# Projections of a second attention: fp16 pairs with power-of-two scales in place of fp32r pairs

## The chip, the cores and the metric

The kernel runs on one NeuronCore of a Trainium2 chip. The metric is the device time of one execution in microseconds. Five engines work side by side and meet at semaphores: TensorE (PE, matmuls, with its weight loads shown apart as PEld), VectorE (DVE), ScalarE (ACT), GpSimd (POOL) and SyncE (SP), whose queue issues most DMAs. Each engine runs its instructions in the order in which they were written.

## What is computed

Three layers follow each other; the change is in the second.

```python
# 1: attention, 2 batches, 8 heads, 768 x 64: a window of 128 keys and 4 sink keys
scores = np.where(is_sink | in_window, scale * q @ k.T, -1e9)
x = softmax(scores) @ v                      # as (2, 768, 512)
# 2: four attention experts of 64 columns, causal, two of them taken per row
logits = x @ w_gate                          # 512 x 4
topk = np.argpartition(-logits, 2, axis=-1)[..., :2]
for e in range(4):
    q, k, v = x @ wq[e], x @ wk[e], x @ wv[e]   # 512 x 64 each
    ye = softmax(causal(q @ k.T / 8)) @ v @ wo[e]
    out += weight(topk == e) * ye
# 3: eight feed-forward experts, one per row, chosen by argmax and a sticky local gate
out[b, s] = p[e] * (np.maximum(x[b, s] @ w1[e], 0) @ w2[e])
```

The order of the logits decides which expert a row takes, so the products must be close to fp32.

## The kernel before

A row tile has 128 rows: 6 tiles in each of the 2 batches. For each tile, layer 1 works head pair by head pair (`p1_unit`): scores on PE, mask and maximum on DVE (L687), exponential on ACT (L697), transposes of P on PE (L721), P split in a high half on ACT (L724) and a low half on DVE (L728), both fp16, and three products with the split V on PE (L736 to L738). From the third tile on, the sink keys get a product of their own, the sink product (L838), fed by small copies (L706). `p1_tail` normalises the tile to x (L859, DVE, out of PSUM), transposes it (L401) and splits it into `xT`, high half on ACT (L407), low half on DVE (L311).

Precision comes from pairs: each operand a is kept as a high half and a low half a - high, and `mm3` (L306 to L308) adds three products: high by high, high by low, low by high. In layer 1 the pairs of P and V are fp16, and V is first scaled by a power of two (`v_scale`, `pow2`). In the projections of layer 2 (`p2_v` for the values and the four gate logits, `p2_qk` for queries and keys) and in layer 3 the pairs are fp32r, which need no scale.

The weights of layer 2 come in three DMAs into two buffers of the ring `wst`, wv, wq, then wk, whose load waits until wv has been read. `weights` splits each: four high halves on ACT (L455), four low halves on POOL (L457, a plain subtraction). DVE takes one maximum, over wv (L448), which with V's bound gives the scale of the projected values (`across`, `pow2`, `p2_scale`).

The order of all instructions is made before anything runs. Each piece of work is a task with an engine, an estimated duration, the tasks it needs, the buffers it takes and a priority; `Order.run` always picks the task that can start earliest, and by priority among equals, and writes it out. Where PE would wait by that plan early in the program, it writes in fill matmuls of 512 columns (L387, `spin`). Layer 2 starts 3.75 tiles after layer 1, so up to then layer 1, the loads and the weights are all there is. POOL makes V's halves for most tiles (L636, L639, L645), DVE and ACT for a few (L625, L629).

The expert weights of layer 3 come through a ring of pairs `w`. Before, its first five buffers were the memory of the layer-2 weights and of `xT`, free once the last projection was through (`spent`); five more and the memory of `wo` came later.

Of the kernel before, what the change touches and what calls it, by code (L numbers as in the profile page):

```python
# [179 lines left out]
D_TR = 0.109  # L180
# [19 lines left out]
def fused_kernel(  # L200
# [48 lines left out]
    front = ExitStack()  # L249
    work = front.enter_context(tc.tile_pool(name="work", bufs=1))  # L250

    x2d = dram.tile([T * C, DM], F32, name="x2d")
    banks = [psum.tile([128, 512], F32, name=f"bank{i}") for i in range(8)]

    def ring(pool, n, name, *tiles):
# [106 lines left out]

    wqk_h = fw.tile([128, KD, 4, 128], FR)
    wqk_l = fw.tile([128, KD, 4, 128], FR)
    wvg_h = fw.tile([128, KD, E1 * D + E1], FR)
    wvg_l = fw.tile([128, KD, E1 * D + E1], FR)
    wo_h = fw.tile([128, 2, XC], FR)
# [62 lines left out]
    def weights(prio):  # L430

        wmax = small.tile([128, KD], F32, name="wmax", bufs=1)
        wgn = fw.tile([128, KD, E1], F32, name="wgn")
        K["wgn"] = add("DMA", 0.5, lambda: nc.sync.dma_start(wgn, w_gate1.rearrange("(p j) e -> p j e", j=KD)), prio=prio)
        g = add("ACT", 0.08, lambda: nc.scalar.activation(wvg_h[:, :, E1 * D:], wgn, AF.Copy), deps=[K["wgn"]], prio=prio)
        K["wg"] = add("POOL", 0.15, lambda: nc.gpsimd.tensor_sub(wvg_l[:, :, E1 * D:], wgn, f32(wvg_h[:, :, E1 * D:])),
                      deps=[g], prio=prio)
        mw = []
        for n, (name, w) in enumerate((("wv", wv), ("wq", wq), ("wk", wk))):
            load("wst", name, 512 * E1 * D * 4, lambda t, w=w: nc.sync.dma_start(  # L440
                t.rearrange("p (e j c) -> p e j c", e=E1, j=KD), w.rearrange("e (p j) c -> p e j c", j=KD)), prio + n)
            dst = [t[:, :, :E1 * D] for t in (wvg_h, wvg_l)] if n == 0 else \
                [t[:, :, 2 * (n - 1):2 * n, :].rearrange("p j m c -> p j (m c)") for t in (wqk_h, wqk_l)]

            def src(name, j):
                return R[name].rearrange("p (e j c) -> p j e c", e=E1, j=KD)[:, j]
            if n == 0:
                mw = [add("DVE", d_v(KD * E1 * D), lambda: nc.vector.tensor_reduce(  # L448
                    wmax[:, 0:1], R["wv"], axis=AX.X, op=OP.max, apply_absolute_value=True), deps=[K["wv"]], prio=prio)]
                K["gw"] = across("gw", lambda: wmax[:, 0:1], mw, prio)  # L450
# [8 lines left out]
            join(ls + (mw if n == 0 else []), [name], prio + n)  # L459
            K[name, "s"] = ls + ([K["wg"]] if n == 0 else [])  # L460
        wov = wo.rearrange("(t e) j c -> t (e j) c", t=2)
# [41 lines left out]

    def across(key, m, deps, prio):

        def a0():
            m1 = small.tile([128, 1], F32, name="amax1")
            nc.vector.reduce_max(m1, m(), axis=AX.X)
            R[key, "m1"] = m1

        def a1():
            nc.tensor.transpose(R[key, "p"][:, :128], R[key, "m1"].to_broadcast([128, 128]), ident)

        def a2():
            g = fw.tile([128, 1], F32, name="max_" + "".join(str(c) for c in key))
            nc.vector.reduce_max(g, R[key, "p"][:, :128], axis=AX.X)
            R[key] = g
        t0 = add("DVE", 0.08, a0, deps=deps, prio=prio)
        t1 = add("PE", D_TR, a1, deps=[t0], acq=[("B", (key, "p"))], prio=prio)
        return add("DVE", 0.2, a2, deps=[t1], rel=[(key, "p")], prio=prio)  # L520

    def pow2(key, m, deps, prio):
        def f():
            s = consts.tile([128, 1], F32, name="s_" + "".join(str(c) for c in key))
            si = consts.tile([128, 1], F32, name="si_" + "".join(str(c) for c in key))
            g = small.tile([128, 1], F32, name="amaxg")
            m(g)
# [5 lines left out]
            R[key] = (s, si)  # L533
        K[key] = add("DVE", 0.95, f, deps=deps, prio=prio)

# [275 lines left out]
    def p1_tail(b, i, prio):  # L811
# [64 lines left out]
    def p2_scale(b, prio):  # L876

        pow2(("sw", b), lambda g: nc.vector.tensor_scalar(g, R["gv", b], R["gw"], float(DM), op0=OP.mult, op1=OP.mult),
             [K["gv", b], K["gw"]], prio)

    def p2_v(b, i, prio):
# [10 lines left out]
        def g():  # L892
            p = R["v2p", b, i]
            nc.scalar.activation(v2[b][0][:, i, :], p[:, :E1 * D], AF.Copy, scale=R["sw", b][0])
            nc.scalar.activation(lg1[b][:, i, :], p[:, E1 * D:E1 * D + E1], AF.Copy)

        def h():
            nc.vector.scalar_tensor_tensor(v2[b][1][:, i, :], R["v2p", b, i][:, :E1 * D], R["sw", b][0], v2[b][0][:, i, :],
                                           op0=OP.mult, op1=OP.subtract)
        t = add("PE", 12 * d_mr(260) + 0.08, f, deps=[K["xT", b, i]] + K["wv", "s"], acq=[("B", ("v2p", b, i))],  # L900
                prio=prio)
        K["v2p", b, i] = t
        K["lg1", b, i] = u = add("ACT", 0.412, g, deps=[t, K["sw", b]], prio=prio)
        K["v2", b, i] = add("DVE", d_v(256) + 0.064, h, deps=[u], rel=[("v2p", b, i)], prio=prio)
# [28 lines left out]
    def p2_qk(b, m, c, prio):  # L933
# [10 lines left out]
        t = add("PE", 12 * d_mr(CH) + 0.07, f, deps=[K["xT", b, i] for i in range(2 * c, 2 * c + 2)] + K["wq" if m < 2 else "wk", "s"],  # L944
                acq=[("B", ("qkp", b, m, c))] + ([("q2", ("q2", b, c))] if m == 0 else []), prio=prio)
# [458 lines left out]
    def sp(u, c, hf, pr=None, ahead=False):  # L1404
# [126 lines left out]
    def unit_end(u):  # L1531
# [232 lines left out]
```

## Time and profile before

| what | value |
|---|---|
| median of 3 runs | 441.61 us (439.83 to 442.22) |
| the profiled execution | 440.41 us |
| its span, first to last instruction | 438.6 us |
| granted TensorE clock, mean | 0.995 |
| PE, DVE, ACT, POOL busy | 420.7, 352.2, 323.1, 129.9 us |
| chain that ended last, by engine | PE 56%, DVE 16%, issue 16%, ACT 6%, DMA 3% |

A busy share is an average over the whole span. Layer 1 starts alone, both attentions run together up to about 217 us, then come the last rows and the routing, and from about 265 us the expert layer. The rows in the section after the change are read stage by stage.

### The profile page before, as it was taken

The page shows a single profiled execution, that of the slowest core. Times are in us where ns is not written, and L with a number is a line of the kernel's source. Part 1 is how long each engine was busy: PE and PEld are TensorE (multiplying, and loading weights), DVE is VectorE, ACT ScalarE, POOL GpSimd, SP SyncE. Part 2 cuts the span into 40 slices and gives each one's busy share as a digit, 9 for nine tenths or more (in the row PEclk, how much of TensorE's full clock was granted, in tenths as well). Part 3 has the DMA queues.
Part 4 walks back from the last instruction along what each step waited for, and adds up shares of the span by engine and source line. Part 5 has one row for each costly group of instructions (what it writes and reads, how often), then busy time and mean ns, then how long its engine had stood idle before and what let it go on. Part 6 is the DMA issues. An engine that isn't in the chain of part 4 may idle for free.

```text
span 438.6 us, 10515 instructions
## 1 busy us (share of the span) xinstructions
PE 420.7 (96%) x3486; PEld 329.7 (75%) x3486; DVE 352.2 (80%) x1019; ACT 323.1 (74%) x759; POOL 129.9 (30%) x214
## 2 busy tenths in 40 slices
PE   8899999999999999999989999999999989999994
PEld 4679988769889779977966767655666767888883
DVE  3999696987889599868879887946779789998690
ACT  5799695975887598768556743936969789899780
POOL 8199921446002024110295104401102033100101
PEclk9999999999999999999999999999999999999999
DMA  8987251210210000100181025778565994100011
GB/s 173 174 189 195 53 118 49 49 50 1 75 50 1 25 2 2 49 1 27 55 315 41 26 73 172 259 240 266 193 212 188 340 390 143 49 26 24 2 50 53
DMA packets 58590, 48.28 MB, mean 110 GB/s; under 512 B 40863, under 2 KB 42399, under 8 KB 58528
## 3 DMA queue, kind: packets, MB, share of 16 engines
q1 hardware_dynamic: 56368, 40.72, 31.7%
q0 software_dynamic: 2160, 6.82, 4.6%
q8 instruction: 29, 0.48, 0.5%
q14 instruction: 33, 0.27, 0.2%
HBM read 86.58 MB, written 6.55 MB: 212 GB/s over the span
## 4 chain that ended last, share of the span: by engine, by line
PE 56%; DVE 16%; issue 16%; ACT 6%; DMA 3%; POOL 2%; SPq 1%; POOLq 0%; another core or an unknown queue 0%; ACTq 0%; DVEq 0%
PE bank L306 9%; PE bank L308 9%; PE bank L307 8%; PE bank L721 7%; PE bank L673 6%; DVE P L687 4%; PE bank L401 3%; DVE pT L728 3%; PE bank L1640 3%; DMA xg<-x2d,gix 2%; PE bank L738 2%; PE bank L736 2%; ACT P L697 2%; PE bank L1442 2%; PE bank L737 2%
## 5 line engine op out<-in xcount | busy, mean ns | idle before, releaser
L697 ACT ACTIVATE P<-P,nm 128x260 f32<-128x260 f32 (+4 forms) x160 | 84.0, 529 | 17.7 <-DVE nm L687 16.0
L728 DVE TENSOR_TENSOR pT<-bank,pT 128x512 f16<-128x512 f32 (+1 forms) x96 | 58.0, 627 | 13.6 <-ACT pT L724 13.1
L1421 DVE TENSOR_TENSOR w<-raw,w 128x1024 fp32r<-128x1024 f32 x44 | 52.9, 1220 | 12.7 <-ACT w L1413 12.4
L724 ACT ACTIVATE pT<-bank 128x512 f16<-128x512 f32 (+1 forms) x96 | 49.1, 550 | 6.8 <-PE bank L721 5.7
L1413 ACT ACTIVATE w<-raw 128x1024 fp32r<-128x1024 f32 x44 | 45.8, 1061 | 8.0 <-DMA raw<-in_moe_w_dram 6.8
L721 PE MATMUL bank<-ident,P 128*128 128x128 f32 x344 | 50.9, 280 | 0.7 <-ACT P L697 0.3
L687 DVE CUSTOM_DVE_ANT_0 P<-bank,mask 128x260 f32<-128x260 f32 (+1 forms) x96 | 36.4, 404 | 8.1 <-PE bank L673 8.0
L721 PEld LDWEIGHTS bank<-ident,P 128*128 128x128 f32 x344 | 38.5, 142 | 4.5 <-ACT P L697 2.4
L736 PEld LDWEIGHTS <-pT 128*128 128x128 f16 x344 | 31.0, 98 | 9.0 <-ACT pT L724 2.4
L1540 POOL DMA_INDIRECT out_dram<-yof,six x12 | 13.8, 1150 | 67.5 <-ACT yof L1537 66.3
L738 PEld LDWEIGHTS <-pT 128*128 128x128 f16 x344 | 30.7, 98 | 4.0 <-DVE pT L728 3.8
L673 PE MATMUL bank<-kT,qT 64*128 64x260 f32 (+1 forms) x192 | 31.2, 408 | 1.9 <-POOL kT L573 1.1
L737 PEld LDWEIGHTS <-pT 128*128 128x128 f16 x344 | 31.2, 99 | 1.1 <-issue 0.3
L697 ACT ACTIVATION_READ_ACCUMULATOR P<-P,nm 128x1 f32 x160 | 31.2, 195 | 0.0
L1462 POOL DMA_INDIRECT xgf<-x2d,gix x9 | 11.2, 1246 | 62.1 <-PE bank L1442 56.6
L306 PE MATMUL bank<-xT,wqk_h 128*128 128x256 f32 x96 | 28.8, 300 | 0.0
L401 PE MATMUL bank<-ident,raw 128*128 128x128 f32 x168 | 28.3, 289 | 0.2
L308 PE MATMUL bank<-xT,wqk_l 128*128 128x256 f32 x96 | 27.1, 282 | 0.0
L307 PE MATMUL bank<-xT,wqk_h 128*128 128x256 f32 x96 | 27.0, 281 | 0.0
L636 POOL TENSOR_SCALAR raw<-raw,s_sv 128x256 f32<-128x256 f32 x20 | 18.7, 946 | 27.1 <-DVE si_sv L532 17.7
L1421 DVE TENSOR_TENSOR xT<-raw,xT 128x1024 fp32r<-128x1024 f32 x17 | 20.6, 1216 | 6.9 <-ACT xT L1413 6.8
L401 PEld LDWEIGHTS bank<-ident,raw 128*128 128x128 f32 x168 | 20.4, 162 | 7.1 <-DVE nm L687 1.7
(444 smaller groups left out, 1319.9 us busy)
## 6 DMA issues: line engine op xcount, KB each, us to landing
raw<-in_moe_w_dram SPq DMA_DIRECT2D x104, 512.0 KB
qw<-in_moe_w_dram SPq DMA_DIRECT2D x64, 256.0 KB
raw<-in_v_dram SPq DMA_DIRECT2D x12, 256.0 KB
x2d<-x SPq DMA_DIRECT2D x12, 256.0 KB
raw<-in_q_dram SPq DMA_DIRECT2D x11, 256.0 KB
raw<-in_k_dram SPq DMA_DIRECT2D x11, 256.0 KB
raw<-in_moe_wv_dram SPq DMA_DIRECT2D x1, 512.0 KB
raw<-in_moe_wq_dram SPq DMA_DIRECT2D x1, 512.0 KB
```

The costliest lines, as they stand in the source:

```text
L306: nc.tensor.matmul(o, l[0], r[0], start=start, stop=False)
L307: nc.tensor.matmul(o, l[0], r[1], start=False, stop=False)
L308: nc.tensor.matmul(o, l[1], r[0], start=False, stop=stop)
L401: nc.tensor.transpose(p[:, j * 128:(j + 1) * 128], src(j), ident)
L673: nc.tensor.matmul(o, l, r, start=True, stop=True)
L687: nc.vector.tensor_tensor_reduce(p, s, sg["mask"], 0.0 if dead and st == 1 else -scale, gr["nm"] if si else 3.0e38, op0=OP.add, op1=OP.min ...
L697: nc.scalar.activation(p, p, AF.Exp, bias=gr["nm"], scale=-1.0, accum_out=sg["sum"]())
L721: nc.tensor.transpose(R[tk][:, j * 128:(j + 1) * 128], R[gr["P"]][:, c:c + 128], ident)
L724: nc.scalar.activation(R[sk_][0][:, :n * 128], R[tk][:, :n * 128], AF.Copy)
L728: nc.vector.tensor_sub(pl[:, :n * 128], R[tk][:, :n * 128], ph[:, :n * 128])
L1413: nc.scalar.activation(R["w", u, c, hf][0], R["raw", u, c, hf], AF.Copy)
L1421: eng.tensor_sub(wl[:, :, s_], R["raw", u, c, hf][:, :, s_], f32(wh)[:, :, s_])
```

## The change

The pairs of `xT` and of the weights wq, wk, wv and w_gate become fp16. That takes four things.

- **Scales.** Each weight gets a power of two from its own largest value (w_gate one of its own, beside wv's): a maximum over each weight on DVE, PE's transpose to bring it across the partitions (`across`, now straight from the column, for one or two columns), and a chain `pow2` each. The high halves on ACT take the scale as a factor; the low halves move from POOL to DVE as one fused operation, weight x scale - high.
- **x keeps V's scale.** The operation that normalises x no longer multiplies by V's inverse scale.
- **Undoing.** `p2_scale` makes small columns of products of the inverse scales, by batch (and, in the first batch, by V's two scales); the evictions of values, logits, queries and keys take them as a factor.
- **Memory.** `xT` and the layer-2 weights lie in a pool of their own, half as large, closed after the last projection (`turnover`). The ring `w` begins with two buffers of its own and gets three more at the turnover; the first conversions on POOL no longer wait for `spent`.

The number of matmuls and their shapes stay. The planner's estimates follow the new types (`d_mh` for `d_mr`, 0.55 for 0.95 for a `pow2`).

```diff
-        "xT": ring(fw, 2, "xT", ([128, KD, 2 * C], FR), ([128, KD, 2 * C], FR)),
+        "xT": ring(wx, 2, "xT", ([128, KD, 2 * C], F16), ([128, KD, 2 * C], F16)),
...
-    wqk_h = fw.tile([128, KD, 4, 128], FR)
+    wqk_h = wx.tile([128, KD, 4, 128], F16)
...
+            mw = add("DVE", d_v(KD * E1 * D), lambda name=name, n=n: nc.vector.tensor_reduce(
+                wmax[:, n + (n > 0):n + (n > 0) + 1], R[name], axis=AX.X, op=OP.max, apply_absolute_value=True), deps=[K[name]], prio=prio + n)
+            t = across(("g", name), lambda cols=cols: wmax[:, cols], [mw] + [mg] * (n == 0), prio + n, 2 if n == 0 else 1)
...
+            pow2(("s", name), lambda g, name=name: nc.vector.tensor_copy(g, R["g", name]), [t], prio + n, 2 if n == 0 else 1)
...
-                h = add("ACT", d_a(E1 * D), lambda name=name, j=j, h_=h_: nc.scalar.activation(h_, src(name, j), AF.Copy),
-                        deps=[K[name]], prio=prio + n)
-                ls.append(add("POOL", d_p(E1 * D), lambda name=name, j=j, h_=h_, l_=l_: nc.gpsimd.tensor_sub(
-                    l_, src(name, j), f32(h_)), deps=[h], prio=prio + n))
+                h = add("ACT", d_a(E1 * D), lambda name=name, j=j, h_=h_: nc.scalar.activation(
+                    h_, src(name, j), AF.Copy, scale=R["s", name][0][:, 0:1]), deps=[K["s", name]], prio=prio + n)
+                ls.append(add("DVE", d_v(E1 * D) + 0.064, lambda name=name, j=j, h_=h_, l_=l_: nc.vector.scalar_tensor_tensor(
+                    l_, src(name, j), R["s", name][0][:, 0:1], h_, op0=OP.mult, op1=OP.subtract), deps=[h], prio=prio + n))
...
-            nc.vector.scalar_tensor_tensor(x, R["O", 1, b, i].rearrange("p (h d) -> p h d", h=H),
-                                           R["se" if i < early(b) else "sv", b][1],
-                                           r[:, :, None].to_broadcast([128, H, D]), op0=OP.mult, op1=OP.mult)
+            nc.vector.tensor_tensor(x, R["O", 1, b, i].rearrange("p (h d) -> p h d", h=H),
+                                    r[:, :, None].to_broadcast([128, H, D]), op=OP.mult)
...
+            def f1(kind=kind, ud=ud):
+                nc.vector.tensor_scalar(ud[:, 0:2], R["s", "wv"][1], R[kind, b][1], None, op0=OP.mult)
+                nc.vector.tensor_mul(ud[:, 0:1], ud[:, 0:1], R["sw", b][0])
...
-        K["qk", b, m, c] = add("ACT", d_a(CH), lambda: nc.scalar.activation(dst(), R["qkp", b, m, c][:, :CH], AF.Copy),
-                               deps=[t] + ([K["qkp", b, 0, c]] if m == 1 else []), rel=[("qkp", b, m, c)], prio=prio)
+        K["qk", b, m, c] = add("ACT", d_a(CH), lambda: nc.scalar.activation(dst(), R["qkp", b, m, c][:, :CH], AF.Copy,
+                                                                            scale=undo(b, 2 * c, 2 + m // 2)),
...
-    bufs["w"] = [tuple(two(t, i) for t in wqk) for i in range(2)] + [(two(flat_(wvg_h)), two(flat_(wvg_l)))]
-    bufs["w"] += [tuple(two(flat_(t)) for t in p) for p in bufs["xT"]]
+    bufs["w"] = ring(fw, 2, "wa", ([128, 2, 512], FR), ([128, 2, 512], FR))
...
+    def turnover():
+        proj.close()
+        early_ = front.enter_context(tc.tile_pool(name="early", bufs=1, side="right", reuse_waits="tile"))
+        bufs["w"] += ring(early_, 3, "wb", ([128, 2, 512], FR), ([128, 2, 512], FR))
```

The planner's order moves with it. On DVE, before, from the end of the chain that makes the scale of the projected values (`s_sw`, `si_sw`) to the normalised x of the second tile (`raw_0_89`, L859) and on into the scores of the third:

```order
L531 TENSOR_SCALAR s_sw_725<-s_sw_725 128x1
L532 TENSOR_SCALAR si_sw_726<-amaxg 128x1
L859 SCALAR_TENSOR_TENSOR raw_0_89<-bank_82,si_se_459,r_0_1_231 128x512
L706 COPY skp_0_133<-P_0_104 128x3x8
L687 ISA P_0_101,nm<-bank_80,mask_172 128x260
```

The same place on DVE now, from the chain for wq's scale (`s_swq`) to the same x (`raw_0_92`, L871 in the new numbering); L460 are the low halves of the weights, L900 undo factors:

```order
L543 TENSOR_SCALAR s_swq<-s_swq 128x1
L544 TENSOR_SCALAR si_swq<-amaxg 128x1
L460 SCALAR_TENSOR_TENSOR wvg_l<-raw_0_86,s_swv,wvg_h 128x256
L900 TENSOR_TENSOR undo_se_233<-si_swq,si_se_469 128x1
L900 TENSOR_TENSOR undo_sv_234<-si_swq,si_sv_610 128x1
L460 SCALAR_TENSOR_TENSOR wvg_l<-raw_0_86,s_swv,wvg_h 128x256 x3
L465 SCALAR_TENSOR_TENSOR wvg_l<-wgn,s_swv,wvg_h 128x4x4
L460 SCALAR_TENSOR_TENSOR wqk_l<-raw_0_87,s_swq,wqk_h 128x256 x4
L871 TENSOR_TENSOR raw_0_92<-bank_85,r_0_1_236 128x512
```

Between the value scale's chain and the second tile's x stand now two more chains, a maximum over wq, the undo factors and nine low halves.

On POOL, before, from the low half of V's second tile (`v_1_98`, L645) on; L457 are the low halves of the weights:

```order
L645 TENSOR_TENSOR v_1_98<-raw_0_85,v_0_97 128x256 x2
L457 TENSOR_TENSOR wvg_l<-raw_0_83,wvg_h 128x256 x4
L457 TENSOR_TENSOR wqk_l<-raw_0_84,wqk_h 128x256 x4
L636 TENSOR_SCALAR raw_0_86<-raw_0_86,s_sv_598 128x256 x2
L639 CAST v_0_99<-raw_0_86 128x512
L645 TENSOR_TENSOR v_1_100<-raw_0_86,v_0_99 128x256 x2
L457 TENSOR_TENSOR wqk_l<-raw_0_83,wqk_h 128x256 x4
```

The same place on POOL now (L648, L651, L657 are L636, L639, L645 of before):

```order
L657 TENSOR_TENSOR v_1_101<-raw_0_88,v_0_100 128x256 x2
L648 TENSOR_SCALAR raw_0_89<-raw_0_89,s_sv_609 128x256 x2
L651 CAST v_0_102<-raw_0_89 128x512
L657 TENSOR_TENSOR v_1_103<-raw_0_89,v_0_102 128x256 x2
L648 TENSOR_SCALAR raw_0_89<-raw_0_89,s_sv_609 128x256 x2
L651 CAST v_0_96<-raw_0_89 128x512
```

The weights are gone from POOL, and V's tiles follow each other without a break.

## Rows read from the trace of the kernel before

**Rows 1.** The page: busy us, share of the span and instructions of each engine.

```profile
PE 420.7 (96%) x3486; PEld 329.7 (75%) x3486; DVE 352.2 (80%) x1019; ACT 323.1 (74%) x759; POOL 129.9 (30%) x214
```

**Rows 2.** Windows: stretch, length, busy us (instructions) by engine, granted clock, DMA share, GB/s.

```profile
core 0: us, PE busy (x) PEld busy (x) DVE busy (x) ACT busy (x) POOL busy (x), PEclk, DMA share, GB/s
20.00:40.00 20.00, 19.51 (x182) 15.88 (x181) 19.29 (x77) 19.26 (x64) 17.08 (x23) 1.00 0.86 200
40.00:60.00 20.00, 20.00 (x245) 18.60 (x245) 15.84 (x61) 15.82 (x51) 16.92 (x24) 1.00 0.36 86
160.00:180.00 20.00, 20.00 (x245) 17.08 (x243) 18.71 (x77) 17.95 (x63) 6.87 (x11) 1.00 0.04 15
31.00:46.00 15.00, 15.00 (x156) 14.40 (x155) 13.28 (x47) 13.74 (x47) 14.69 (x21) 1.00 0.59 148
```

**Rows 3.** PE in order of time: start, us, line, operands, shape, count.

```profile
26.84 1.03 PE L387 MATMUL bank<-v2h 128*128 128x512 f16 x4
29.16 0.81 PE L387 MATMUL bank<-v2h 128*128 128x512 f16 x3
31.53 1.04 PE L721 MATMUL bank<-ident,P 128*128 128x128 f32 x8
61.40 0.19 PE L736 MATMUL bank<-v,pT 128*128 128x64 f16 x1
61.43 0.19 PE L737 MATMUL bank<-v,pT 128*128 128x64 f16 x1
65.08 0.28 PE L306 MATMUL bank<-xT,wqk_h 128*128 128x256 f32 x1
66.03 0.28 PE L308 MATMUL bank<-xT,wqk_l 128*128 128x256 f32 x1
```

**Rows 4.** DVE in order of time, the operations that price the added ones.

```profile
13.96 0.68 DVE L585 TENSOR_REDUCE vmax<-raw 128x1 f32<-128x512 f32 x1
14.56 0.74 DVE L629 SCALAR_TENSOR_TENSOR v<-raw,s_se,v 128x512 f16<-128x512 f32 x1
20.56 0.29 DVE L516 TENSOR_REDUCE max_gv<-bank 128x1 f32<-128x128 f32 x1
21.36 0.14 DVE L595 COPY amaxg<-max_gv 128x1 f32<-128x1 f32 x1
22.25 0.68 DVE L311 TENSOR_TENSOR xT<-bank,xT 128x512 fp32r<-128x512 f32 x1
24.93 1.22 DVE L448 TENSOR_REDUCE wmax<-raw 128x1 f32<-128x1024 f32 x1
```

**Rows 5.** DVE beside POOL: order of time, and durations (ns, min/median/max) by line.

```profile
40.36 2.83 POOL L457 TENSOR_TENSOR wqk_l<-raw,wqk_h 128x256 fp32r<-128x256 f32 x4
41.14 0.72 DVE L923 TENSOR_TENSOR g_eq<-g_eq,tri 128x32 f32<-128x32 f32 x1
L923 DVE TENSOR_TENSOR g_eq<-g_eq,tri x6: 174/184/717, 41.1 to 212.4; 128x32 f32<-128x32 f32 x6
78.17 1.23 DVE L629 SCALAR_TENSOR_TENSOR v<-raw,s_sv,v 128x512 f16<-128x512 f32 x1
L636 POOL TENSOR_SCALAR raw<-raw,s_sv x20: 912/922/1357, 22.4 to 133.3; 128x256 f32<-128x256 f32 x20
```

**Rows 6.** DVE in order of time: waits of the first weights' stretch, idle before in brackets.

```profile
45.61 0.17 DVE L489 COPY wog<-bank 128x9 f32<-128x9 f32 x1 [0.73 <-PE bank L482]
46.50 0.17 DVE L489 COPY wog<-bank 128x9 f32<-128x9 f32 x1 [0.72 <-PE bank L482]
48.61 0.75 DVE L859 SCALAR_TENSOR_TENSOR raw<-bank,si_sv,r 128x512 f32<-128x512 f32 x1 [1.94 <-PE bank L838]
```

**Rows 7.** ACT groups: busy us, mean ns, idle before; with a scale and without.

```profile
L894 ACT ACTIVATE v2h<-bank,s_sw 128x256 f16<-128x256 f32 x12 | 5.5, 462 | 0.0
L947 ACT ACTIVATE k<-bank 128x256 f32<-128x256 f32 x12 | 4.6, 384 | 14.2 <-PE bank L308 14.2
```

**Rows 8.** Windows of PE alone around a wait for a gather: busy us (instructions), granted clock.

```profile
225.00:229.00 4.00, 2.26 (x20) 0.99 0.81 278
229.00:232.50 3.50, 3.50 (x25) 0.52 0.47 178
```

More of the change, by code (lines that the diff above doesn't have):

```diff
@@ L250, in fused_kernel @@
     work = front.enter_context(tc.tile_pool(name="work", bufs=1))
+    proj = ExitStack()
+    wx = proj.enter_context(tc.tile_pool(name="wx", bufs=1, side="right"))
     x2d = dram.tile([T * C, DM], F32, name="x2d")
@@ L430, in weights @@
     def weights(prio):
-        wmax = small.tile([128, KD], F32, name="wmax", bufs=1)
+        wmax = small.tile([128, 4], F32, name="wmax", bufs=1)
         wgn = fw.tile([128, KD, E1], F32, name="wgn")
         K["wgn"] = add("DMA", 0.5, lambda: nc.sync.dma_start(wgn, w_gate1.rearrange("(p j) e -> p j e", j=KD)), prio=prio)
[L435 to L438, printed above, removed]
+        mg = add("DVE", 0.09, lambda: nc.vector.tensor_reduce(
+            wmax[:, 1:2], wgn.rearrange("p j e -> p (j e)"), axis=AX.X, op=OP.max, apply_absolute_value=True), deps=[K["wgn"]], prio=prio)
         for n, (name, w) in enumerate((("wv", wv), ("wq", wq), ("wk", wk))):
@@ L501, in weights, with across @@
         join([K["wos", t] for t in range(2)] + [a], ["wo"], prio + 2)
-    def across(key, m, deps, prio):
+    def across(key, m, deps, prio, n=0):
         def a0():
@@ L511, in a1, with pow2 @@
         def a1():
-            nc.tensor.transpose(R[key, "p"][:, :128], R[key, "m1"].to_broadcast([128, 128]), ident)
+            for j in range(max(n, 1)):
+                col = m()[:, j:j + 1] if n else R[key, "m1"]
+                nc.tensor.transpose(R[key, "p"][:, j * 128:(j + 1) * 128], col.to_broadcast([128, 128]), ident)
         def a2():
-            g = fw.tile([128, 1], F32, name="max_" + "".join(str(c) for c in key))
-            nc.vector.reduce_max(g, R[key, "p"][:, :128], axis=AX.X)
+            w = max(n, 1)
+            g = fw.tile([128, w], F32, name="max_" + "".join(str(c) for c in key))
+            nc.vector.reduce_max(g, R[key, "p"][:, :128 * w].rearrange("p (n c) -> p n c", n=w), axis=AX.X)
             R[key] = g
[L518 to L522, printed above, removed]
+        t0 = deps if n else [add("DVE", 0.08, a0, deps=deps, prio=prio)]
+        t1 = add("PE", D_TR * max(n, 1), a1, deps=t0, acq=[("B", (key, "p"))], prio=prio)
+        return add("DVE", 0.2 * max(n, 1), a2, deps=[t1], rel=[(key, "p")], prio=prio)
+    def pow2(key, m, deps, prio, n=1):
         def f():
-            s = consts.tile([128, 1], F32, name="s_" + "".join(str(c) for c in key))
-            si = consts.tile([128, 1], F32, name="si_" + "".join(str(c) for c in key))
-            g = small.tile([128, 1], F32, name="amaxg")
+            s = consts.tile([128, n], F32, name="s_" + "".join(str(c) for c in key))
+            si = consts.tile([128, n], F32, name="si_" + "".join(str(c) for c in key))
+            g = small.tile([128, 2], F32, name="amaxg")[:, :n]
             m(g)
@@ L533, in f @@
             R[key] = (s, si)
-        K[key] = add("DVE", 0.95, f, deps=deps, prio=prio)
+        K[key] = add("DVE", 0.55, f, deps=deps, prio=prio)
     def halves(b, i):
@@ L876, in p2_scale, with f2, undo, undone @@
     def p2_scale(b, prio):
-        pow2(("sw", b), lambda g: nc.vector.tensor_scalar(g, R["gv", b], R["gw"], float(DM), op0=OP.mult, op1=OP.mult),
+        pow2(("sw", b), lambda g: nc.vector.tensor_scalar(g, R["gv", b], R["g", "wv"][:, 0:1], float(DM), op0=OP.mult, op1=OP.mult),
              [K["gv", b], K["gw"]], prio)
+        for kind in (["se"] if early(b) else []) + ["sv"]:
+            ud = small.tile([128, 4], F32, name=f"undo_{kind}{b}", bufs=1)
+            R["undo", b, kind] = ud
+            def f1(kind=kind, ud=ud):
+                nc.vector.tensor_scalar(ud[:, 0:2], R["s", "wv"][1], R[kind, b][1], None, op0=OP.mult)
+                nc.vector.tensor_mul(ud[:, 0:1], ud[:, 0:1], R["sw", b][0])
+            def f2(m, kind=kind, ud=ud):
+                nc.vector.tensor_mul(ud[:, 2 + m:3 + m], R["s", "wk" if m else "wq"][1], R[kind, b][1])
+            K["undo", b, kind, 0] = add("DVE", 0.14, f1, deps=[K["sw", b], K[kind, b], K["s", "wv"]], prio=prio)
+            for m in range(2):
+                K["undo", b, kind, 1 + m] = add("DVE", 0.07, lambda m=m, f2=f2: f2(m), deps=[K[kind, b], K["s", "wk" if m else "wq"]], prio=prio + 1)
+    def undo(b, i, n):
+        kind = "se" if i < early(b) else "sv"
+        return R["undo", b, kind][:, n:n + 1]
+    def undone(b, i, n):
+        return K["undo", b, "se" if i < early(b) else "sv", n]
     def p2_v(b, i, prio):
@@ L1422, in sp @@
         after = [K["ga", 1]] if u == 0 and (c, hf) == (3, 1) else []
-        h = K["wh", u, c, hf] = add("POOL" if ahead else "ACT", 1.06 if ahead else d_a(1024) + 0.055, hi, deps=[K["ld", u, c, hf]] + (spent + [K["routed", JE]] * c if ahead else [K.get(("wh", 0, 1, 1))] * (u == 0 and c == 2)),
+        h = K["wh", u, c, hf] = add("POOL" if ahead else "ACT", 1.06 if ahead else d_a(1024) + 0.055, hi, deps=[K["ld", u, c, hf]] + ([K["routed", JE]] * c if ahead else [K.get(("wh", 0, 1, 1))] * (u == 0 and c == 2)),
                                     acq=[("w", ("w", u, c, hf))], prio=pr)
```

38 lines of the change are left out of this document (23 added, 15 removed).

## The prediction

> **What bounds the kernel now.** I read the page's busy shares first, then the table of windows, then VectorE (DVE) and TensorE (PE) in order of time around 10 to 50 us. On the page PE is busy 96% of the span [rows 1], but that says nothing on the stage that the change touches. The windows split it [rows 2]. From 40 to 60 and from 160 to 180 us PE is busy all 20.00 us, DVE 15.84 and 18.71: there PE is the bound, and a matmul that gets shorter is worth its whole saving. From 20 to 40 us DVE has 19.29 and ScalarE (ACT) 19.26 of 20 us: there whatever is added to them pushes the rest. The change takes PE time out of the first kind of stretch and puts DVE work into the second, so the two are priced apart.
>
> **What it takes from PE.** The projections are 12 value products and 24 query and key products of 12 matmuls each, 432 in all. From 65.08 to 66.03 us nine fp32r matmuls in a row start 0.12 us apart [rows 3]. No fp16 matmul of 256 columns is in the trace. The nearest are the fill matmuls of 512 columns (three take 0.81 us, four 1.03: 0.22 each) and the 64-column products of the attention, 0.03 us apart, each with a weight load of its own, so the load of 128 columns doesn't hold them [rows 3]. A line through both, 0.03 + 192 x 0.00042, gives 0.11 for 256 columns. So 0.01 is saved on each, 4.3 us in all. The bounds are 0, if something else than the type sets the 0.12, and 0.013 each, if an fp16 matmul goes by its columns alone (half of 0.22 less the rounding). I take 0.01, and of the 432 only those that run where PE is the bound: 72 (two value and four query and key products) lie in the stretch that DVE will hold up, the other 360 save 3.6 us.
>
> The rows give 0.22 per fp16 matmul of 512 columns. The Trainium skill (TensorE: Matmul & The Clock Gate, Back-to-back issue gap) gives 81 ns at 128 columns and 131 ns at 512 as the sustained spacing with a weight load each; an estimate between these two figures is 98 ns at 256, by which 360 matmuls would save 7.9 us and the sum below would be +0.9. At 512 columns the row is far above 131 ns, so the row decides.
>
> **What it adds to DVE.** Before, GpSimd (POOL) made the low halves of the weights; now DVE does, and takes the maxima and makes the scales. Counted from the order, priced by the durations of DVE in order of time [rows 4] (each operation starts about 0.08 us before the one ahead of it ends, 13.96 + 0.68 against 14.56):
> - two more maxima over a 1024-wide weight tile, 1.22 us each: 2.4
> - three more power-of-two chains of six one-column operations, 0.89 us from 21.36 to 22.25: 2.7
> - maxima over three more transposed columns, 0.29 less the overlap: 0.6
> - eight small operations for the undo factors, 0.07 to 0.19 each as in the chain: 0.9
> - twelve low halves of 256 columns. The 512-column form (L629 at 14.56) takes 0.74 less 0.08; 512 columns more cost a maximum 0.54 (1.22 against 0.68), so 256 fewer save 0.27: 0.39 each, 4.7.
>
> That is 11.3 us, and it all stands ahead of the attention output of the third tile (L859, at 48.61 us before [rows 6]). The DVE pieces in the section on the change show it: from the scale chain to the output of the second tile there was nothing, now there are two more chains, nine low halves and more. PE gets 14 more fill matmuls there (39 against 25 up to the first sink product): the useful work waits for DVE.
>
> What takes it up: DVE stood idle three times there until PE was through, 0.73 + 0.72 + 1.94 = 3.4 us [rows 6]; that goes first. And PE works ahead: up to the first sink product it has now done 12 transposes more, 0.11 each (eight take 1.04 [rows 3]), 1.3 us. 11.3 - 3.4 - 1.3 = 6.6.
>
> **The shared port.** DVE beside POOL in order of time shows POOL in DVE's way [rows 5]. From 40.36 to 43.19 POOL runs four weight subtractions end to end. DVE's small two-input operation of the gate at 41.14 takes 0.72 us and ends as the second of them ends; the same line has a median of 184 ns over the program and a maximum of 717. The change works both ways here. It removes the 12 subtractions. Some 16 such short operations (sink copies, gate) stand in the stretch, held by up to 0.53 each; half of that is 4 us that could come back. But POOL's preparation of V moves up into the gap (POOL has 14.69 of 15 us from 31 to 46 us [rows 2]), and the order puts four tiles of it there back to back, so I count 1.0. Against it, the twelve new DVE operations and the gate's all read two SBUF tiles. The one row of that form beside POOL work is L629 at 78.17: 1.23 us, 0.49 more than 0.74, while POOL's next operation is held in turn (at most 1357 ns, median 922). The bounds for thirteen are 0 and a whole POOL operation of 0.75 each, 9.8; the row would give 6.4. I take half of it, 3.2: the key weights' four come late, perhaps after POOL's work, and no row shows several in succession.
>
> That row has a hold of 0.49. The Trainium skill (SBUF — State Buffer, Who interferes with whom) says that a DVE instruction with two SBUF inputs contends with a GpSimd one that reads SBUF, and that the second to issue is blocked until the first is through. Strictly taken it would be the upper bound, 9.8 in place of 3.2; that is the fourth case below.
>
> **Smaller edits.** A scale from a tensor makes ACT's evictions longer: 462 ns with it, 384 without [rows 7]. 24 query and key evictions, 12 of the logits and 13 weight pieces make 49 x 0.08 = 3.9 us of ACT. From 40 us on ACT is busy 79 to 90% [rows 2] and this lies beside PE's work; the weights' 1.0 us lies beside DVE's longer stretch. Cost 0, up to 1. The x output loses one factor but still reads PSUM at a pass an element: 0. On SP's queue the loads of wk and wo now wait for DVE's last read of wv and wq, with a key tile and V tiles behind them; the maximum over wk stands on DVE behind the second split of x, long after its load: 0. The expert stage has as many weight buffers as before, split in another way, two of them free earlier; its loads are not moved: 0, by 1 us either way.
>
> **Sum.** 6.6 - 1.0 + 3.2 - 3.6 = +5.2 us. The profiled execution took 440.41 us for a span of 438.6, so 445.6 for one like it; the median of the runs shown is 441.61, 1.2 above it, which gives 446.8.
>
> **The rivals**, all on that median. A measurement of this kernel tells about 0.5%, 2.2 us, from no change.
> - *A, the forecast (0.45):* DVE is late in the first 50 us, with some holds at the port: 442.5 to 450.5, middle 446.8.
> - *B, they cancel (0.22):* the new operations are not held and 4 us come back: 6.6 - 4.0 - 3.6 = -1.0, 440.6. For it: POOL must let DVE in between two of its operations; against it: L629's row.
> - *C, faster (0.17):* its place is DVE from 25 to 48 us, its mechanism that POOL's subtractions were what made DVE slow there. If two thirds of the possible holds go, 5.5 us, no new ones come and a matmul saves 0.013: 6.6 - 5.5 - 4.7 = -3.6, 438.0. It decides once DVE reaches the third tile's output less than 4.9 us (3.6 + 1.3) later than before. Against it: V's preparation reads SBUF as the subtractions did, and stands in their place.
> - *D, far slower (0.11):* every new operation waits out one of POOL's, 9.8, and PE, starved meanwhile, loses its clock: from 225 to 229 us PE was busy 2.26 of 4 us, and from 229 to 232.5 the granted clock is 0.52 [rows 8], near the lower of its two levels, 1.2 of 2.4 GHz; half of 3.5 us is 1.7. 6.6 - 1.0 + 9.8 + 1.7 - 3.6 = +13.5, 455.1.
> - *E, the matmuls don't get shorter (0.05):* 0.12 stays, as for fp32r: 6.6 - 1.0 + 3.2 = +8.8, 450.4.
>
> **How the numbers follow.** A, D and E are slower by over 0.5%: 0.61. B is within: 0.22. C is faster: 0.17. The time is A's, 446.8. The range leaves out the lower part of C and most of D: 439.5 to 452.5. The slower cases alone would have 442.5 to 455.
>
> **What would show it.** The output of the third tile comes at 55 to 61 us in place of 48.61. The new low halves take 0.47 us where POOL is idle and up to 1.2 beside it. Projection matmuls start 0.11 apart. PE is full again right after, the first gather for the experts comes about 5 us later than before, and the stage behind it is as it was. I am wrong if PE stays full from 31 to 46 us (15.00 of 15.00 before [rows 2]), or if the spacing is under 0.10.

## The result, and the profile after

The changed kernel takes 445.31 us (median of 6 runs, 444.78 to 447.92), the kernel before 441.61 beside it: ratio 1.010, 95% interval 1.006 to 1.014. It is slower by about 4.5 us, inside the forecast. The profiled execution has a span of 446.1 us (before 438.6); it is the longest of its runs, so a second trace of the same kernel, 443.2 us long and the shortest of its ten, is read beside it.

The page and the windows of the first trace, against [rows 1, 2]:

```profile
PE 423.1 (95%) x3503; PEld 322.7 (72%) x3503; DVE 363.6 (81%) x1066; ACT 327.3 (73%) x759; POOL 122.7 (27%) x201
```

```profile
20.00:40.00 20.00, 16.93 (x142) 11.28 (x140) 19.38 (x71) 13.36 (x36) 16.07 (x19) 0.93 0.67 151
40.00:60.00 20.00, 19.11 (x216) 16.54 (x215) 18.39 (x73) 16.59 (x48) 9.44 (x14) 0.98 0.56 116
31.00:46.00 15.00, 11.59 (x74) 7.80 (x73) 14.55 (x48) 9.44 (x27) 14.54 (x19) 0.89 0.71 171
160.00:180.00 20.00, 19.96 (x260) 15.72 (x260) 19.32 (x66) 18.09 (x58) 5.64 (x9) 1.00 0.04 15
36.00:42.00 6.00, 3.93 (x21) 2.58 (x21) 6.00 (x16) 3.16 (x10) 5.85 (x7) 0.72 0.35 102
246.00:250.00 4.00, 4.00 (x29) 3.23 (x27) 3.86 (x13) 3.79 (x12) 0.00 (x0) 0.63 0.01 4
```

From 31 to 46 us PE is busy 11.59 us instead of 15.00, ACT 9.44 instead of 13.74, and DVE goes up to 14.55: DVE is the bound there, and the others wait for it. At 160 us PE is as full as before. Two stretches at a lower granted clock, 0.72 and 0.63, stand out. These are means over a stretch: from 38 to 40 us the clock is 0.50, the lower of its two levels (1.2 of 2.4 GHz). The second trace has the same idle time and neither stretch:

```profile
31.00:46.00 15.00, 11.13 (x85) 7.51 (x82) 14.59 (x49) 10.17 (x28) 14.08 (x17) 1.00 0.79 174
36.00:42.00 6.00, 4.22 (x30) 2.99 (x30) 6.00 (x18) 3.15 (x9) 5.78 (x7) 1.00 0.59 142
246.00:250.00 4.00, 3.96 (x55) 3.10 (x54) 3.80 (x11) 4.00 (x13) 0.00 (x0) 1.00 0.02 4
```

DVE in order of time in the first trace, the new work (before: [rows 4, 6]):

```profile
31.25 0.47 DVE L453 COPY amaxg<-max_gwv 128x2 f32<-128x2 f32 x1
31.75 0.41 DVE L540 TENSOR_SCALAR amaxg<-amaxg 128x2 f32<-128x2 f32 x1
34.51 0.15 DVE L540 TENSOR_SCALAR amaxg<-amaxg 128x1 f32<-128x1 f32 x1
36.13 1.26 DVE L460 SCALAR_TENSOR_TENSOR wvg_l<-raw,s_swv,wvg_h 128x256 f16<-128x256 f32 x3
37.60 2.42 DVE L460 SCALAR_TENSOR_TENSOR wqk_l<-raw,s_swq,wqk_h 128x256 f16<-128x256 f32 x4
39.95 0.68 DVE L871 TENSOR_TENSOR raw<-bank,r 128x512 f32<-128x512 f32 x1
47.89 1.68 DVE L460 SCALAR_TENSOR_TENSOR wqk_l<-raw,s_swk,wqk_h 128x256 f16<-128x256 f32 x4
59.58 0.69 DVE L871 TENSOR_TENSOR raw<-bank,r 128x512 f32<-128x512 f32 x1
```

The second tile's x comes at 39.95 instead of 29.37 us, the third's at 59.58 instead of 48.61 [rows 6]. The second tile's before:

```profile
29.37 0.75 DVE L859 SCALAR_TENSOR_TENSOR raw<-bank,si_se,r 128x512 f32<-128x512 f32 x1
```

The chain for wv's two scales (from 31.25) takes 1.80 us; the chains for wq and wk, 0.89 and 0.88. What PE and ACT do meanwhile, in order of time:

```profile
31.69 2.54 PE L389 MATMUL bank<-v2h 128*128 128x512 f16 x11
34.06 0.60 PE L403 MATMUL bank<-ident,raw 128*128 128x128 f32 x4
37.51 0.37 PE L308 MATMUL bank<-wvg_h,xT 128*128 128x260 f16 x1 [2.84 <-ACT qT L409]
```

```profile
33.10 1.71 ACT L458 ACTIVATE wvg_h<-raw,s_swv 128x256 f16<-128x256 f32 x4 [2.50 <-DVE s_swv L543]
35.27 1.70 ACT L458 ACTIVATE wqk_h<-raw,s_swq 128x256 f16<-128x256 f32 x4 [0.26 <-DVE s_swq L543]
36.88 0.57 ACT L409 ACTIVATE qT<-bank 128x512 f32<-128x512 f32 x1
```

PE runs 11 fills in a row, four transposes, and is idle for 2.84 us. ACT is idle for 2.50 us until the scale of wv is there, and the query's eviction (L409) stands in its queue behind the high halves of wv and wq.

The span splits at the first gather for the experts. On POOL before, in the first trace after and in the second:

```profile
218.15 1.21 POOL L1462 DMA_INDIRECT xg<-x2d,gix  x1 [1.40 <-DVE no L1268]
```

```profile
223.45 1.21 POOL L1492 DMA_INDIRECT xg<-x2d,gix  x1 [2.09 <-DVE no L1300]
```

```profile
222.63 1.21 POOL L1492 DMA_INDIRECT xg<-x2d,gix  x1 [2.09 <-DVE no L1300]
```

The gather is 5.3 and 4.5 us late. Behind it, up to the end of the span, lie 220.4 us before, 222.7 in the first trace after and 220.5 in the second. So the loss is in the front. The 2.2 us behind it in the first trace are not in the second, so the change alone doesn't bring them.

### The profile page after: what moved, and what is told of

Same layout as the page of the kernel before. It is cut to its first block, busy times and chain, and to the rows that moved or that the text cites. A ratio compares the mean times of both kernels' runs of the same rounds, so it can differ in the third digit from the quotient of the medians.

```text
span 446.1 us, 10614 instructions
## 1 busy us (share of the span) xinstructions
PE 423.1 (95%) x3503; PEld 322.7 (72%) x3503; DVE 363.6 (81%) x1066; ACT 327.3 (73%) x759; POOL 122.7 (27%) x201
## 4 chain that ended last, share of the span: by engine, by line
PE 51%; DVE 17%; issue 16%; DMA 6%; ACT 5%; SPq 2%; POOL 2%; POOLq 0%; another core or an unknown queue 0%; ACTq 0%; DVEq 0%
PE bank L308 8%; PE bank L310 8%; PE bank L309 7%; PE bank L685 7%; PE bank L733 6%; DVE pT L740 4%; DMA raw<-in_moe_w_dram 4%; DVE P L699 3%; PE bank L403 3%; PE bank L1677 2%; PE bank L750 2%; PE bank L748 2%; PE bank L749 2%; DMA qw<-in_moe_w_dram 1%; SPq L1667 1%
## 5 line engine op out<-in xcount | busy, mean ns | idle before, releaser
L1451 DVE TENSOR_TENSOR wb<-raw,wb 128x1024 fp32r<-128x1024 f32 x25 | 30.3, 1219 | 8.6 <-ACT wb L1443 8.5
L685 PE MATMUL bank<-kT,qT 64*128 64x260 f32 (+1 forms) x192 | 30.2, 409 | 1.2 <-issue 1.1
L1443 ACT ACTIVATE wb<-raw 128x1024 fp32r<-128x1024 f32 x25 | 26.4, 1062 | 2.6 <-DMA raw<-in_moe_w_dram 1.3
L648 POOL TENSOR_SCALAR raw<-raw,s_sv 128x256 f32<-128x256 f32 x20 | 19.0, 960 | 33.1 <-DVE si_sv L544 22.8
L699 DVE CUSTOM_DVE_ANT_0 P<-bank,cmask 128x384 f32<-128x384 f32 (+3 forms) x48 | 24.3, 527 | 4.4 <-PE bank L685 4.3
L308 PE MATMUL bank<-xT,wqk_h 128*128 128x256 f16 x96 | 26.2, 273 | 0.3 <-DVE wog L497 0.3
```

The costliest lines, as they stand in the source:

```text
L308: nc.tensor.matmul(o, l[0], r[0], start=start, stop=False)
L685: nc.tensor.matmul(o, l, r, start=True, stop=True)
L699: nc.vector.tensor_tensor_reduce(p, s, sg["mask"], 0.0 if dead and st == 1 else -scale, gr["nm"] if si else 3.0e38, op0=OP.add, op1=OP.min ...
L1443: nc.scalar.activation(R["w", u, c, hf][0], R["raw", u, c, hf], AF.Copy)
L1451: eng.tensor_sub(wl[:, :, s_], R["raw", u, c, hf][:, :, s_], f32(wh)[:, :, s_])
```

## Experiments

The prediction's theory: DVE's added work, less what is taken up, costs more than the shorter matmuls give. The rivals: the loss is somewhere else (expert buffers, the planner's order, ACT's wait), the matmuls give nothing, POOL's subtractions had slowed DVE. A time difference below is a ratio times 441.6.

### All of the new work, fp32r operands

```diff
-    wqk_h = wx.tile([128, KD, 4, 128], F16)
+    wqk_h = fw.tile([128, KD, 4, 128], FR)
...
-    bufs["w"] = ring(fw, 2, "wa", ([128, 2, 512], FR), ([128, 2, 512], FR))
+    bufs["w"] = [tuple(two(t, i) for t in wqk) for i in range(2)] + [(two(flat_(wvg_h)), two(flat_(wvg_l)))]
```

> The changed kernel with its projection operands back in fp32r and the expert buffers of before, and all of the new work on the weights (maxima, scales, DVE low halves) kept. If the shorter matmuls are what the change gains, the projections start 0.12 us apart again and the time is that of the changed kernel plus about 4.3 us: 445.3 + 4.3 = 449.6, ratio to before about 1.018. If the type gains nothing on the path (rival E), it stays at 445. If the new expert buffers cost the 2 us that the stage behind the first gather has become longer in the profile after, it would be 447.5 and that stage as short as before.

Measured: 454.99 us, ratio 1.032 (1.028 to 1.036): +14.1. So the fp16 operands, with the buffers and the order that go with them, are worth some 10 us beside this work, over twice what was expected. Up to the first gather it is 8.0 (230.62 against 222.63). The other 3.6 lie behind the gather, where there are no projections: this trace is the longest of its four and has a granted clock of 0.79 from 246 to 254 us, so part of them is this execution's, and the rest may be the buffers' or the order's. PE in order of time, here and in the second trace after, shows what the type changes:

```profile
73.34 0.37 PE L306 MATMUL bank<-wvg_h,xT 128*128 128x260 f32 x1
73.55 0.28 PE L307 MATMUL bank<-wvg_l,xT 128*128 128x260 f32 x1
73.67 0.28 PE L308 MATMUL bank<-wvg_h,xT 128*128 128x260 f32 x1
```

```profile
71.31 0.27 PE L308 MATMUL bank<-wvg_h,xT 128*128 128x260 f16 x1
71.42 0.27 PE L309 MATMUL bank<-wvg_l,xT 128*128 128x260 f16 x1
71.53 0.27 PE L310 MATMUL bank<-wvg_h,xT 128*128 128x260 f16 x1
```

Within a group the starts are 0.12 and 0.11 apart. But the first interval of an fp32r group is 0.21, of an fp16 group 0.11.

### fp16 operands without the new work

The weights are not scaled here: POOL subtracts as before the change, and one maximum is left.

```diff
...
-                    h_, src(name, j), AF.Copy, scale=R["s", name][0][:, 0:1]), deps=[K["s", name]], prio=prio + n)
-                ls.append(add("DVE", d_v(E1 * D) + 0.064, lambda name=name, j=j, h_=h_, l_=l_: nc.vector.scalar_tensor_tensor(
-                    l_, src(name, j), R["s", name][0][:, 0:1], h_, op0=OP.mult, op1=OP.subtract), deps=[h], prio=prio + n))
...
+                    h_, src(name, j), AF.Copy, scale=1.0), deps=[K[name]], prio=prio + n)
+                ls.append(add("POOL", d_p(E1 * D), lambda name=name, j=j, h_=h_, l_=l_: nc.gpsimd.tensor_sub(
+                    l_, src(name, j), h_), deps=[h], prio=prio + n))
```

> The changed kernel's fp16 projections and nothing of its work on the weights: unscaled fp16 high halves on ACT, all twelve low halves on GpSimd as before the change, one maximum, no scales of the weights. Against the version with fp32r operands and all of that work (455.0) the fp16 operands were worth 9.7 us. If that gain doesn't depend on the work beside it: 441.4 - 9.7 = 431.7, and at least 434 by what the matmuls' starts alone give (7.2 us to the first gather). If the planner's new order or the moved buffers are what costs, and not DVE's work: 438 to 442, near the version with the fixed scale and GpSimd's low halves (441.7).

Measured: 437.35 us, ratio 0.991 (0.987 to 0.9945): -4.1, faster than both kernels, but short of the 431.7 expected. Its first gather:

```profile
214.97 1.21 POOL L1481 DMA_INDIRECT xg<-x2d,gix  x1 [1.72 <-DVE no L1289]
```

That is 3.2 us ahead of before. The intervals from one projection start to the next sum to 55.1 us before and 48.0 here. The short intervals ahead of the groups grow from 1.2 to 2.0 in all, so PE saves 6.3. Half of it arrives at the gather. (This trace is the shortest of its ten; 2.0 us of its lead lie behind the gather.) So what the type gives depends on what stands beside it: 4.1 us alone, about 10 beside the new work. The new work costs 8.3 us on fp16 operands (from -4.1 to +4.2, the mean of the two measurements of the change) and 14.1 on fp32r.

### A fixed scale, and POOL's subtractions back

A constant 2^10 instead of the maxima over wq, wk and w_gate and the three chains; the weights' own scale is left out:

```diff
-            pow2(("s", name), lambda g, name=name: nc.vector.tensor_copy(g, R["g", name]), [t], prio + n, 2 if n == 0 else 1)
...
-                    l_, src(name, j), R["s", name][0][:, 0:1], h_, op0=OP.mult, op1=OP.subtract), deps=[h], prio=prio + n))
+                    l_, src(name, j), WS, h_, op0=OP.mult, op1=OP.subtract), deps=[h], prio=prio + n))
```

> The changed kernel without the choice of the weights' scales: a fixed 2^10 stands in place of three maxima (2 x 1.21 and 0.17 us), their 0.42 + 0.28 + 0.27 us over the transposed columns, the three power-of-two chains (1.80 + 0.89 + 0.89) and about 1 us of undo operations; the twelve low halves stay on DVE. If DVE's work ahead of the second and third tile is the cause, about 7.5 us of it goes, ACT no longer waits 2.5 us for the first scale, the first projection starts at or before 35 us, PE has no idle stretch of 2.8 us and no half clock there: 438.5, between 437 and 441. If the low halves and their holds at the port are the larger part, 443 to 445. If the loss lies behind the first gather, 443.

Measured: 442.69 us, ratio 1.0007 (0.997 to 1.005): +0.3, some 4 us less than the changed kernel for about 7.5 us less of DVE work, of which wk's 2.2 stand where it had idle time and wv's low halves now meet POOL. Then wq's and wk's low halves back on POOL, unscaled:

```diff
+                if n:
+                    ls.append(add("POOL", d_p(E1 * D), lambda name=name, j=j, h_=h_, l_=l_: nc.gpsimd.tensor_sub(
+                        l_, src(name, j), h_), deps=[h], prio=prio + n))
+                    continue
```

> As the one with the fixed scale, and the eight low halves of wq and wk go back to GpSimd (subtractions of unscaled weights, as before the change); the value weights' stay on DVE. If DVE's time is all that counts, 8 x 0.45 = 3.6 us of DVE go, 1 to 2 of them on the path: 437. If GpSimd's subtractions were what slowed DVE (rival C), it is slower than the fixed scale alone by 1 to 4 us: 440 to 443.

Measured: 441.72 us, ratio 1.002 (0.999 to 1.005), not to be told from the fixed scale alone. Eight low halves less on DVE and eight subtractions more on POOL cancel within the noise, and this run doesn't part the two. But the version above has all its subtractions on POOL and is the fastest of all: they don't have to go for the kernel to get faster (rival C). What they cost is not shown. What is left on DVE is wv's low halves and the gate's, and they now fall beside POOL's sink values. DVE, and POOL, in order of time:

```profile
24.89 1.08 DVE L467 SCALAR_TENSOR_TENSOR wvg_l<-wgn,wvg_h 128x16 f16<-128x16 f32 x1
27.72 2.12 DVE L462 SCALAR_TENSOR_TENSOR wvg_l<-raw,wvg_h 128x256 f16<-128x256 f32 x2
```

```profile
24.90 1.03 POOL L623 TENSOR_TENSOR vbd<-vk,bdm 96x512 f32<-96x512 f32 x1
28.35 1.21 POOL L626 TENSOR_TENSOR vbd<-vbd,vbd 32x512 f16<-32x512 f32 x1
```

A 16-column operation takes 1.08 us, as long as the POOL operation beside it; the next two low halves take 0.83 and 1.37 us, where one takes 0.41 at its shortest. These five, with the four undo operations, occupy about 4.7 us; the version without scales, above, has all of them but two undo operations off DVE and is 5.0 us faster (from +0.9 to -4.1). By this pair, each microsecond of DVE at this place is about one of the whole.

### The planner's estimate

```diff
-        K[key] = add("DVE", 0.55, f, deps=deps, prio=prio)
+        K[key] = add("DVE", 0.95, f, deps=deps, prio=prio)
```

> The changed kernel with the planner's estimate for a power-of-two chain at 0.95 us as before the change, not 0.55 (the trace has 0.89 to 1.80). The work is the same and only the order moves. If the planner's too short estimate is what lets ACT wait 2.5 us for the scale and hold the query's evictions behind it, the stretch from 31 to 46 us gets fuller and the time falls by 1 to 3 us: 442.5 to 444.5. If the work itself is the cause, it stays within 1 us: 444.5 to 446.

Measured: 447.62 us, ratio 1.0145 (1.010 to 1.019). It doesn't get faster; the first gather is at 223.89, 0.4 and 1.3 us later than in the two traces of the changed kernel. The too short estimate is not the cause. It also shows what an order alone can do to this kernel: up to some 2 us. Every version here has an order of its own, so a difference of that size between two of them is no measure of the work.

### DVE's time by itself, at two places, and ACT's wait

Six maxima over weight tiles that nobody reads, in the kernel before: three each behind wv and wq; the same with ACT's high halves planned behind them; and all six behind wk.

```diff
+            dm = []
+            for i in range(3 if n < 2 else 0):
+                dm.append(add("DVE", d_v(KD * E1 * D), lambda name=name, c=3 * n + i: nc.vector.tensor_reduce(
+                    dmx[:, c:c + 1], R[name], axis=AX.X, op=OP.max, apply_absolute_value=True), deps=[K[name]], prio=prio + n))
```

> The kernel before with six more maxima over 1024-wide weight tiles on DVE, three behind the load of wv and three behind that of wq, 1.13 us each, 6.8 in all, that nothing waits for but the release of the two tiles. By the prediction's term, DVE's idle time (3.4) and PE's working ahead (1.3) take up 4.7 us: +2.1, 443.5. If nothing is taken up: +6.8, 448.2. The version with all of the change's work and no fp16 was 13.6 us slower for 13.9 us of DVE, which speaks for the second.

Measured: 447.42 us, ratio 1.016 (1.006 to 1.026): +7.0 for 6.8 us of DVE, with bounds of +2.6 and +11.3. The prediction's +2.1 lies below them: most of the work is not taken up. The first gather is at 223.83, 5.7 us late, and DVE shows the place:

```profile
27.91 3.46 DVE L454 TENSOR_REDUCE dmx<-raw 128x1 f32<-128x1024 f32 x3
33.55 1.21 DVE L454 TENSOR_REDUCE dmx<-raw 128x1 f32<-128x1024 f32 x1
38.45 0.73 DVE L864 SCALAR_TENSOR_TENSOR raw<-bank,si_se,r 128x512 f32<-128x512 f32 x1
```

The second tile's x is at 38.45, 9.1 us later than before. PE is busy all the while: the planner wrote in 48 fills up to the gather, 25 before, and they alone account for 5.4 us of the 5.7 by which the gather is late. They stand in for a wait, since DVE is full from the first tile's x to the second's (stretch, length, DVE busy, granted clock, DMA share, GB/s):

```profile
19.54:38.45 18.91, 18.64 (x54) 1.00 0.82 181
```

> As the one with six more maxima, and ACT's high halves of wv and of wq now wait for the three of their own tile, as they wait for the scale in the changed kernel. If DVE's time alone is the cost, it is the same within 1 us. If the wait stands in ACT's queue ahead of the query's evictions and so stops PE, it is 2 to 4 us slower than without the wait.

```diff
-                        deps=[K[name]], prio=prio + n)
+                        deps=[K[name]] + dm, prio=prio + n)
```

Measured: 447.01 us, ratio 1.013 (1.005 to 1.021): +5.8, the first gather at 222.70. But the edit did not make ACT wait. It set the order of the plan alone, and the trace shows high halves that start before the maxima of their tile are through. DVE, then ACT:

```profile
28.82 1.21 DVE L454 TENSOR_REDUCE dmx<-raw 128x1 f32<-128x1024 f32 x1
30.89 3.46 DVE L454 TENSOR_REDUCE dmx<-raw 128x1 f32<-128x1024 f32 x3
```

```profile
28.37 1.34 ACT L460 ACTIVATE wvg_h<-raw 128x256 fp32r<-128x256 f32 x4
32.99 1.33 ACT L460 ACTIVATE wqk_h<-raw 128x256 fp32r<-128x256 f32 x4
```

So this is the same DVE work in a second order, with the gather 4.6 us late instead of 5.7, and no run tests ACT's wait by itself. Up to the second tile's x the first trace of the changed kernel speaks against it: from the maximum over wq on, DVE is busy for 10.29 of 10.77 us and waits there for no other engine, so ACT's 2.50 us can't be what holds the x up. What they cost behind it is open.

```profile
29.18:39.95 10.77, 10.29 (x36) 0.88 0.49 116
```

> The kernel before with the same six maxima (6.8 us of DVE) on the weight tile of wk: the order puts all six right ahead of the two copies of the folded gate, where DVE stood idle three times in the trace before (0.73 + 0.72 + 1.94 us), and behind the second tile's output. If it is the place that decides, and DVE's work ahead of the second tile's output comes through whole while this place takes work up: 442 to 445, at least 2 us less than with the maxima on wv and wq (447.4). If DVE's time costs the same anywhere in the first 50 us: 447 to 449.

Measured: 442.94 us, ratio 1.002 (0.998 to 1.007): +1.0 for the same 6.8 us. DVE, and the only wait of PE that is new there:

```profile
40.19 6.85 DVE L454 TENSOR_REDUCE dmx<-raw 128x1 f32<-128x1024 f32 x6
50.37 0.74 DVE L864 SCALAR_TENSOR_TENSOR raw<-bank,si_sv,r 128x512 f32<-128x512 f32 x1
```

```profile
51.16 1.19 PE L401 MATMUL bank<-ident,raw 128*128 128x128 f32 x8 [1.00 <-DVE raw L864]
```

Here PE has projections to do and DVE had idle time; the third tile's x is 1.8 us late, the first gather too (219.96), and the time hardly moves. With the same amount of work, the place decides.

### Everything one tile later

```diff
-LAG = 3.75
+LAG = 4.75
...
-WPR = 0.65
+WPR = 1.65
```

> The changed kernel with all its work, the weights and the second attention one tile later in the planner's order (LAG 4.75 for 3.75, WPR 1.65 for 0.65): the second tile's output comes ahead of wq's maximum and of all low halves. If the work's place is the cause, the second tile's output is near 31 us instead of 39, PE has no idle stretch of 2.8 us, and the time falls by 2 to 5 us: 440.5 to 443.5. If DVE is full either way up to 60 us and only the amount counts, or the second attention misses the tile at the far end: 445 to 448.

Measured: 451.10 us, ratio 1.018 (1.010 to 1.025). The second tile's x comes at 29.46 as meant, but the work now stands ahead of the third tile, whose x comes at 62.6, and PE waits there for the same chain, with a clock of 0.50 from 36 to 42 us:

```profile
33.93 0.43 PE L523 MATMUL bank<-ident,wmax 128*128 128x128 f32 x1 [1.87 <-DVE wmax L448]
35.88 1.12 PE L403 MATMUL bank<-ident,raw 128*128 128x128 f32 x4 [1.52 <-DVE xT L313]
39.16 0.40 PE L308 MATMUL bank<-wvg_h,xT 128*128 128x260 f16 x1 [2.17 <-DVE max_gwq L528]
```

The run also changes the far end: the first gather comes at 234.95, and only 214.4 us lie behind it. It moves the block of work without spreading it, so it doesn't tell how the work would do in small pieces.

### The changed kernel again

> The changed kernel once more, for a second trace: 445.3 within 1 us. If the first trace's half clock from 36 to 42 us and from 243 to 250 us belong to the kernel, they come again, with PE idle from 34 to 37 us; the first gather is near 222.8 (the 0.7 us that the first trace lost ahead of 15 us, in the first loads, need not come again).

Measured: 445.72 us, ratio 1.009 (1.005 to 1.0125). PE is idle for 2.83 us at the same instruction, but the clock stays at 1.00. The lower clock follows the idle time in one execution and not in another.

## Why the prediction came right, step by step

**The time** came out 1.5 us under the forecast, the direction is A's. Put together from what the runs show, the terms below make 2.2 us less than the forecast's sum (3.0 for 5.2), and the measured rise is about 1.2 above that, so part of the nearness is luck.

**PE's saving.** The spacing of 0.11 is right. The saving per matmul was too small: it was read inside a group [rows 3], and the first interval of an fp32r group, 0.21, was not looked at. 31 groups at 0.09 are 2.8 us, less some 0.8 that the interval ahead of a group grows. It grows behind fp32 transposes, from 0.03 to 0.11: there the two intervals make 0.23 with fp32r and 0.22 with fp16, and hardly anything is won. Behind the 64-column fp16 products they make 0.23 and 0.14. PE saves 6.3, not 4.3. Of that 4.1 arrive without the new work, where 3.6 were counted; where the rest goes is not shown.

**DVE's added work.** 11.3 plus 3.2 of holds were forecast; the added operations occupy 13.9 us in the first trace (15.3 by their lines, of which before had 1.4). The part for the holds was sized well and put in the wrong place. Of the low halves only three of twelve were held, by 0.17, 0.35 and 0.41; two of them are wq's (first trace after, durations in ns, min/median/max):

```profile
L460 DVE SCALAR_TENSOR_TENSOR wqk_l<-raw,s_swq,wqk_h x4: 472/650/885, 37.6 to 39.1; 128x256 f16<-128x256 f32 x4
```

About 0.9 went to wv's chain, whose operations have two columns: 0.41 at 31.75, and 0.15 at 34.51 with one column and POOL as busy. Two columns where POOL is idle take 0.17 in the same trace:

```profile
54.76 0.17 DVE L960 TENSOR_SCALAR g_mx<-g_mx 128x2 f32<-128x2 f32 x1
```

Three of the chain's six operations were that long; the other three took 0.15 to 0.22. The prediction priced it like the one-column chain. The Trainium skill (SBUF — State Buffer, Who interferes with whom) lists copies and tensor-scalar operations among those that can take the shared pair in a two-port mode; these rows agree for three of the five such operations, and the prediction had read only its line on two inputs. That the second to issue waits out the first agrees in direction: POOL's scaling took 1.47 us beside the low halves of wv, 0.92 in the median.

**The relief** was put at 1.0 and was nearer to 2.8 (an estimate, since not the same old operations lie in the stretch). DVE's durations from 20 to 60 us, above what the same form takes when free, sum to 5.0 us before and 4.5 and 4.8 in the two traces after; with about 2.4 of new holds among them, as much and a little more of the old ones went. The whole port term, +2.2 in the sum, was about -0.4.

**What is taken up** (4.7) is the step whose mechanism was wrong. DVE's idle time [rows 6] was counted against all of the added work. It lies behind the second tile. Of the 6.8 us of maxima put there 1.8 arrive at the gather; of the same 6.8 ahead of the second tile 5.7 and 4.6 arrive. In the changed kernel wk's part stands behind the second tile: its maximum, chain, undo factors and low halves, 4.0 us. What stands ahead of it mostly comes through. That the size was nearly right is luck: wk's part happens to be about as large as the idle time and the 1.3 us of PE's working ahead, which no run prices, together.

**Together:** 13.9 - 4.0 - 2.8 - 4.1 = +3.0 against a measured 4.5 and 3.9. The rest, about 1.2, isn't assigned, and it is larger if part of the work ahead of the second tile was taken up as well. Nor is it settled why the type gives more beside the new work (about 10) than alone (4.1): 3.6 of the difference lie behind the first gather, and that version's trace has a granted clock of 0.79 from 34 to 42 and from 246 to 254 us. No run separates these.

**The rivals.** C wanted the third tile's x less than 4.9 us late; it is 11.0 late. E falls with the spacing. D's lower clock came in the first trace, and 0.28 of 6 us are its price of 1.7. But almost none of it reached the gather: the first projection starts 0.70 us later than in the second trace, ahead of the slow matmuls, and the gather comes 0.82 later. Whether the lower clock from 246 to 250 us made the 2.2 us behind the gather is not shown. B did not come, but the fixed scale ends where it would have.

**What was to be seen:** the third tile's x at 59.58 (55 to 61 forecast), low halves at 0.47 alone and up to 0.89 beside POOL, a spacing of 0.11, the gather 5.3 and 4.5 us later, and in the second trace the stage behind it unchanged. All of it came, except that PE was not full right after: 19.11 of 20 us from 40 to 60. Of the smaller edits priced at nothing, the expert buffers cost nothing in the second trace; ACT's longer evictions were not tested by themselves.

## What to carry to other kernels

Idle time of an engine pays only for work that can stand where the idle time is. Before you subtract it, look at which instruction ends it and on which side of that the new work will be. And price a matmul group with its first interval and the one ahead of it: what a change of kind costs between two matmuls is not seen inside a group, and it depends on what stands ahead.

If the weights' range allows, fp16 pairs without scales of their own gave 0.991 here: the gain was in the matmuls, the loss in the work that prepared them.

## What the hardware showed that was not expected

- An fp32r group begins with an interval of 0.21 us, in nearly all of its 31 groups; an fp16 group doesn't. The interval from an fp32 transpose to an fp32r matmul is 0.03, to an fp16 matmul 0.11, so that behind transposes the two kinds come out nearly even (0.23 and 0.22).
- Two columns instead of one made tiny DVE operations slow beside POOL: 0.41 against 0.15 us, and 0.17 with two columns and POOL idle.
- The same idle stretch of PE, 2.84 and 2.83 us, was followed by a lower clock (0.72 over 6 us) in one execution and by none in the other.
